# Output weights loaded in 4 KB rows, four matrix rows to a partition, with selection matmuls ahead of the output product

## The chip, the cores and the metric

The kernel runs on one core of a Trainium2 chip. The metric is the device time of one execution in microseconds (us). Before the change it is 1385.94 us, the median of three runs (1384.96 to 1386.25).

## The reference, cut to what matters

Two attention operators for one new token, batch 4, head size 128, outputs side by side:

```python
# A: 32 query heads on 8 key/value heads, the last W = 2048 of 8192 keys of the cache
q = x @ wq                      # 4 x 512 by 512 x 4096
p = softmax(q . k / sqrt(128))  # per batch and head
o = p @ v
out_A = o.reshape(4, 4096) @ wo # wo: 4096 x 512, bf16
# B: the same with 32 query heads on 32 key/value heads and 8192 keys
out = concatenate([out_A, out_B], axis=-1)   # 4 x 1 x 1024
```

Nearly all of the bytes are the caches of B: 2 x 4 x 32 x 8192 x 128 elements of 2 bytes, 537 MB of the 588 MB that the kernel reads. The two `wo` matrices, which the change is about, are 4.2 MB each.

## The kernel before

The work is cut into 72 chunks: 8 of A (one for each key/value head; K and V 2 MB each) and 64 of B (two heads of one batch; K and V 4 MB each). For each chunk TensorE transposes K in groups of eight tiles, multiplies them with q, and later multiplies the probabilities with V. One queue issues all loads in a fixed order: K of the next chunk, V of this one, and a `wo` piece of four heads (512 KB) where one is due. A load is issued when its place in memory is free. A `wo` piece goes into one of three slots:

```python
def dma_wo(i):
    ab, wg = (0, i) if i < Hkv else (1, i - Hkv)
    slot = i % NWO                                   # NWO = 3
    src = WO[ab][wg * 4 * P:(wg + 1) * 4 * P, :].rearrange("(hl d) n -> d hl n", d=P)
    dst = wor[:, slot, :].rearrange("p (hl n) -> p hl n", hl=4)
    waits = [("wos" if i - NWO >= Hkv else "fin", wo_last[i - NWO])] if i >= NWO else []
    sch.add_dma("sp", lambda e: e.dma_start(dst, src), "d_wo%d" % slot, waits=waits, key=("wo", i))
```

In this form partition d gets row d of each of the four heads, in four rows of 1 KB. The output product can then use a head's output as it lies:

```python
def emit_fin(c):
    ...
    if ab == 1:
        ov = oz[:, :].rearrange("p (b u) -> p b u", u=2)
        ops = [(ov[:, :, u], wos[:, u, :]) for u in range(2)]
    else:
        ...
        ops = [(ov[:, :, cc], w[:, cc, :]) for cc in range(REP)]   # REP = 4
    ...                                      # one 512-column matmul for each of ops, into fin
```

Where the product stands among the groups of the next chunks:

```python
def keys_part(c):
    ...
    for g in range(ch["NG"]):                # 8 groups in A, 16 in B
        emit_T(ch["s"] + g)                  # eight transposes; VectorE or ScalarE copies them out
        if g >= SLAG:
            emit_S(ch["s"] + g - SLAG)       # eight score matmuls
        if 1 <= c <= NCA and g == 2:
            stats_gmax(c - 1)
        if 1 <= c <= NCA and g == 3:
            stats_exp(c - 1)                 # VectorE, then ScalarE: exponentials
        if 1 <= c <= NCA and g == 6:
            norm_sum(c - 1)
        if 2 <= c <= NCA + 1 and g == 4:
            emit_fin(c - 2)                  # A: four matmuls
        ...
        if c > NCA + 2 and (c - NCA) % 2 == 1 and g == 4:
            emit_fin(c - 2)                  # B: two matmuls
```

Of the kernel before, what the change touches and what calls it, by code (L numbers as in the profile page):

```python
# [9 lines left out]
BF16 = mybir.dt.bfloat16  # L10
# [12 lines left out]
LASTV = (64, 32, 16, 16)  # L23

TRM0, BC0, L0, Q0, XT0 = 0, 256, 288, 320, 448


class _Sched:
# [88 lines left out]
def bass_concat_heads__sliding_block_cached__mha_block_cached__decode_kernel(  # L117
# [53 lines left out]
    with ExitStack() as es:  # L171
# [7 lines left out]

        kv = sb("kv", [P, NH, 8192], BF16)  # L180
        kt = sb("kt", [P, NKT, TG * P], BF16)
        wos = sb("wos", [P, 2, DO], BF16)
        qb = sb("qb", [P, 2, NW], BF16)
        wor = sb("wor", [P, NWO, 4 * DO], BF16)
        xs = sb("xs", [NB, 2, D], BF16)
# [27 lines left out]

        semnames = ["eng_pe", "eng_dve", "eng_act", "eng_pool", "d_x0", "d_x1", "d_o0", "d_o1"]
        semnames += ["d_h%d" % i for i in range(NH)] + ["d_vl%d" % i for i in range(len(LASTV))]
        semnames += ["d_wo%d" % i for i in range(NWO)]
        sems = {n: es.enter_context(nc.semaphore(n)) for n in semnames}


# [40 lines left out]
        def dma_wo(i):  # L260
            ab, wg = (0, i) if i < Hkv else (1, i - Hkv)
            slot = i % NWO
            src = WO[ab][wg * 4 * P:(wg + 1) * 4 * P, :].rearrange("(hl d) n -> d hl n", d=P)
            dst = wor[:, slot, :].rearrange("p (hl n) -> p hl n", hl=4)
            waits = [("wos" if i - NWO >= Hkv else "fin", wo_last[i - NWO])] if i >= NWO else []
            sch.add_dma("sp", lambda e: e.dma_start(dst, src), "d_wo%d" % slot, waits=waits, key=("wo", i))

# [34 lines left out]
        wo_next = 0  # L302
        for kind, c in loads:
            dma_kv(kind, c)
            if kind == "v":
                while wo_next < NWOL and wo_first[wo_next] <= c:
                    dma_wo(wo_next)
                    wo_next += 1
# [47 lines left out]

        idv = identf[:, :].rearrange("p (x b) -> p b x", b=NB)
        sch.add("dve", lambda e: e.tensor_reduce(out=mk[:, :], in_=idv, axis=AX.X, op=ALU.add), waits=["c_identf"], key="mk")


        def tile_of(kind, c, j):
# [183 lines left out]

        def emit_wos(c):

            h = 2 * chunks[c]["hp"] % 4
            w = wor[:, chunks[c]["wo"] % NWO, :].rearrange("p (hl n) -> p hl n", hl=4)
            sch.add("dve", lambda e: e.tensor_copy(wos[:, :, :], w[:, h:h + 2, :]),  # L550
                    waits=[("wo", chunks[c]["wo"])] + ([("fin", c - 2)] if c - 2 >= NCA else []), key=("wos", c))

        def emit_fin(c):
            ch = chunks[c]
            ab = ch["ab"]
            p0 = 0 if ab == 1 else 32
            if ab == 1:
                ov = oz[:, :].rearrange("p (b u) -> p b u", u=2)
                ops = [(ov[:, :, u], wos[:, u, :]) for u in range(2)]
                waits = [("oT", c), ("wos", c)]  # L560
            else:
                w = wor[:, ch["wo"] % NWO, :].rearrange("p (hl n) -> p hl n", hl=4)
                ov = oT[:, c % NSM, :].rearrange("p (u c) -> p u c", c=REP)
                ops = [(ov[:, :, cc], w[:, cc, :]) for cc in range(REP)]
                waits = [("oT", c), ("wo", ch["wo"])]
            lastc = NC - 1 if ab == 1 else NCA - 1
            for i, (l, r) in enumerate(ops):
                pe_mm(fin[p0:p0 + NB, :], l, r, start=i == 0 and c == 0, stop=i == len(ops) - 1 and c == lastc,
                      waits=waits if i == 0 else [], key=("fin", c) if i == len(ops) - 1 else None)
            if c == lastc:  # L570
                sch.add("dve", lambda e: e.tensor_copy(outsb[p0:p0 + NB, :], fin[p0:p0 + NB, :]), waits=[("fin", c)], key=("osb", ab))
                sch.add_dma("sp" if ab == 1 else "act",
                            lambda e: e.dma_start(out[:, 0, ab * DO:(ab + 1) * DO], outsb[p0:p0 + NB, :]),
                            "d_o%d" % ab, waits=[("osb", ab)], key=("out", ab))
# [6 lines left out]
        def keys_part(c):  # L581
            ch = chunks[c]
            if c >= NCA and (c - NCA) % 2 == 0:
                sch.mark()
            for g in range(ch["NG"]):
                emit_T(ch["s"] + g)
                if g >= SLAG:
                    emit_S(ch["s"] + g - SLAG)
# [4 lines that stand above are left out]
                    stats_exp(c - 1)  # L593
                if 1 <= c <= NCA and g == 6:
                    norm_sum(c - 1)
                if 2 <= c <= NCA + 1 and g == 4:
                    emit_fin(c - 2)
                if c > NCA + 1 and (c - NCA) % 2 == 0 and g == 4:
                    emit_wos(c - 1)
                if c > NCA + 1 and (c - NCA) % 2 == 0 and g == 6:  # L600
                    norm_sum(c - 1)
                if c > NCA + 2 and (c - NCA) % 2 == 1 and g == 4:
                    emit_fin(c - 2)

        def values_part(c, nxt):
# [31 lines left out]
                pe_mm(fin[0:NB, :], qb[:, 0, 0:NB], pbt[0][:, 1, 0:DO], stop=False, waits=["c_qb", ("c_pb", 0)])  # L637
            values_part(c - 1 if c else None, c)
        sch.mark()
        emit_wos(NC - 1)  # L640
        norm_sum(NC - 1)
        for g in range(chunks[NC - 1]["NG"]):
            emit_pv(NC - 1, g)
# [58 lines left out]
```

## Time and profile before

| | before |
|---|---|
| time, median of 3 | 1385.94 us |
| span of the profiled execution | 1384.5 us |
| bytes, mean rate | 587.80 MB, 425 GB/s |
| last K block lands | 1358.60 us |
| from there to the end | 25.9 us |

The views that bound the kernel stand in the prediction. The page's line of busy times adds how much room the engines have:

```profile
PE 1173.0 (85%) x26769; PEld 1130.0 (82%) x26769; DVE 643.2 (46%) x1326; ACT 436.1 (31%) x649; POOL 4.1 (0%) x14
```

TensorE is at 85%. It is no bound over the whole run.

### The profile page before, as it was taken

How to read it: one execution, taken by the hardware profiler on the slowest of the kernel's cores; microseconds unless marked ns; L12 is line 12 of the kernel's file. 1: busy time of each engine (PE TensorE's matmuls, PEld its weight loads, DVE VectorE, ACT ScalarE, POOL GpSimd, SP SyncE). 2: the span in 40 equal slices, each digit the busy share in tenths (PEclk: the TensorE clock that was granted, in tenths of full speed). 3: DMA queues.
4: the chain of work that ended last, by engine and by line, in shares of the span. 5: the costliest groups of instructions: out<-in, count | busy, mean ns of one | idle time of the engine just before them, and what ended most of it. 6: DMA issues, size and time to landing. Idle time of an engine off the chain costs nothing.

```text
span 1384.5 us, 57099 instructions
## 1 busy us (share of the span) xinstructions
PE 1173.0 (85%) x26769; PEld 1130.0 (82%) x26769; DVE 643.2 (46%) x1326; ACT 436.1 (31%) x649; POOL 4.1 (0%) x14
## 2 busy tenths in 40 slices
PE   4888888898888788988889788888898888888888
PEld 4777878897888788887889788887798888887887
DVE  1566444454444444444444444444454445444443
ACT  1554323333223322332233233332233233322332
POOL 1000000000000000000000000000000000000000
PEclk9899999999999999999999999999999999999998
DMA  9999999999999999999999999999999999999996
GB/s 400 414 417 422 426 428 430 434 425 437 427 436 427 432 430 434 429 425 436 427 436 427 435 427 436 426 428 435 429 434 430 433 427 435 428 429 432 431 434 255
DMA packets 29979, 587.80 MB, mean 425 GB/s; under 512 B 2656, under 2 KB 10864, under 8 KB 11120
## 3 DMA queue, kind: packets, MB, share of 16 engines
q1 hardware_dynamic: 29912, 587.22, 99.2%
q8 instruction: 27, 0.44, 0.1%
q14 instruction: 16, 0.13, 0.0%
q10 hardware_dynamic: 24, 0.01, 0.0%
HBM read 587.21 MB, written 0.01 MB: 424 GB/s over the span
## 4 chain that ended last, share of the span: by engine, by line
DMA 66%; PE 31%; DVE 1%; issue 1%; ACT 0%; SPq 0%; ACTq 0%; DVEq 0%
DMA kv<-in_B_k_cache_dram 64%; PE tr L321 19%; PE sc L323 9%; DMA kv<-in_B_wq_dram 2%; PE fin L323 2%; PE po L323 1%; PE ms L323 1%; DVE sA L430 1%; DVE kt L383 0%; DVE rm L439 0%; DVE sA L428 0%; ACT pba L493 0%; PE ms L321 0%; ACT kt L381 0%; ACT pbb L478 0%
## 5 line engine op out<-in xcount | busy, mean ns | idle before, releaser
L321 PE MATMUL tr<-identb,kv 128*128 128x128 bf16 x8704 | 702.7, 231 | 171.7 <-DMA kv<-in_B_k_cache_dram 169.0
L383 DVE COPY kt<-tr 128x1024 bf16<-128x1024 bf16 x736 | 502.6, 691 | 484.5 <-PE tr L321 480.4
L321 PEld LDWEIGHTS tr<-identb,kv 128*128 128x128 bf16 x8704 | 557.7, 105 | 197.4 <-issue 128.6
L381 ACT ACTIVATE kt<-tr 128x1024 bf16<-128x1024 bf16 x352 | 360.2, 1024 | 638.1 <-PE tr L321 635.0
L323 PE MATMUL sc<-qb,kt 128*128 128x64 bf16 x8192 | 424.6, 197 | 1.7 <-issue 1.5
L323 PEld LDWEIGHTS sc<-qb,kt 128*128 128x128 bf16 x8192 | 350.8, 101 | 3.9 <-issue 1.6
L323 PE MATMUL po<-pbb,kv 128*128 128x64 bf16 (+1 forms) x8192 | 289.9, 192 | 5.5 <-issue 5.5
L323 PEld LDWEIGHTS po<-pbb,kv 128*128 128x128 bf16 x8192 | 263.3, 97 | 7.6 <-issue 5.8
L478 ACT ACTIVATE pbb<-sc,negb 64x128 bf16<-64x128 f32 x128 | 51.2, 400 | 296.8 <-DVE negb L468 296.0
L444 DVE TENSOR_REDUCE rm<-sc 64x1 f32<-64x128 f32 x128 | 37.0, 289 | 94.2 <-PE sc L323 93.3
L456 DVE TENSOR_REDUCE gm<-ms 1x2 f32<-1x128 f32 (+1 forms) x72 | 20.1, 279 | 44.6 <-PE ms L321 44.5
L468 DVE COPY negb<-ms 128x1 f32<-128x1 f32 (+1 forms) x72 | 11.4, 159 | 55.4 <-PE ms L323 55.4
L323 PE MATMUL sc<-qs,kt 128*128 128x64 bf16 (+3 forms) x512 | 26.6, 198 | 10.8 <-DVE kt L383 10.5
L323 PEld LDWEIGHTS sc<-qs,kt 128*128 128x128 bf16 x512 | 21.8, 102 | 13.2 <-DVE kt L383 11.8
L323 PE MATMUL ms<-identf,gx 1*128 1x1 f32 (+1 forms) x144 | 27.8, 260 | 0.6 <-DVE gx L460 0.6
L323 PEld LDWEIGHTS ms<-identf,gx 1*128 1x128 f32 (+1 forms) x144 | 21.7, 188 | 4.9 <-DVE gx L460 0.8
L478 ACT ACTIVATION_READ_ACCUMULATOR pbb<-sc,negb 64x1 f32 x128 | 23.7, 185 | 0.0
L321 PE MATMUL ms<-identf,rm 128*1 128x128 f32 (+1 forms) x72 | 19.8, 275 | 0.2 <-DVE rm L444 0.2
L323 PE MATMUL fin<-wos,oz 128*4 128x512 bf16 x64 | 19.5, 386 | 0.3 <-DVE oz L542 0.3
L323 PE MATMUL po<-pba,kv 128*128 128x64 bf16 x512 | 18.9, 193 | 0.0
L460 DVE TENSOR_SCALAR gx<-gm 1x128 f32<-1x128 f32 (+1 forms) x72 | 15.9, 221 | 2.5
L323 PEld LDWEIGHTS po<-pba,kv 128*128 128x128 bf16 x512 | 16.6, 98 | 0.0
(47 smaller groups left out, 155.5 us busy)
## 6 DMA issues: line engine op xcount, KB each, us to landing
kv<-in_B_k_cache_dram SPq DMA_DIRECT2D x64, 4096.0 KB, 27.7
kv<-in_B_v_cache_dram SPq DMA_DIRECT2D x63, 4096.0 KB, 32.5
kv<-in_A_k_cache_dram SPq DMA_DIRECT2D x8, 2048.0 KB, 27.4
kv<-in_A_v_cache_dram SPq DMA_DIRECT2D x8, 2048.0 KB, 26.6
kv<-in_A_wq_dram SPq DMA_DIRECT2D x1, 4096.0 KB, 12.3
kv<-in_B_wq_dram SPq DMA_DIRECT2D x1, 4096.0 KB, 27.3
wor<-in_A_wo_dram SPq DMA_DIRECT2D x8, 512.0 KB, 23.6
wor<-in_B_wo_dram SPq DMA_DIRECT2D x8, 512.0 KB, 33.6
```

The lines of the kernel that those rows point to most:

```text
L321: emit = lambda e: e.transpose(o, l, r)
L323: emit = lambda e: e.matmul(o, l, r, start=start, stop=stop)
L381: sch.add("act", lambda e: e.activation(dst, src, ACTF.Copy), waits=waits, key=("ev", s))
L383: sch.add("dve", lambda e: e.tensor_copy(dst, src), waits=waits, key=("ev", s))
L430: emit = lambda e, src=src, b=b: e.scalar_tensor_tensor(out=t, in0=src, scalar=mk[:, b:b + 1], in1=t, op0=ALU.mult, op1=ALU.add)
L444: sch.add("dve", lambda e, src=src, pp=pp: e.tensor_reduce(out=rm[pp, m, 0:1], in_=src, axis=AX.X, op=ALU.max), waits=[("S", ch["s_last"]) ...
L456: sch.add("dve", lambda e: e.tensor_reduce(out=gm[0:C, m, 0:U], in_=src, axis=AX.X, op=ALU.max), waits=[("trm", c)], key=("gmax", c))
L460: sch.add("dve", lambda e: e.tensor_scalar(out=dst, in0=gv, scalar1=-scale, scalar2=None, op0=ALU.mult), waits=[("gmax", c)], key=("gx", c))
L468: sch.add("dve", lambda e: e.tensor_copy(negb[:, m, 0:C], ms[:, col:col + C]), waits=[("bc", c)], key=("negb", c))
L478: sch.add("act", lambda e, src=src, pp=pp, n=n, u=u: e.activation(pbv[pp, :, u], src, ACTF.Exp, bias=negb[pp, m, 0:1], scale=scale, accum_ ...
```

## The change

The intent: `wo` in rows of 4 KB instead of 1 KB, so that the same bytes cost fewer packets. Partition p then holds rows 4p to 4p+3 of a piece of four heads, so a partition no longer belongs to one position within a head. The head outputs are put in that order by four selection matmuls (0/1 matrices built from the identity) and small VectorE copies. The diff, cut to its core:

```diff
+        wos = sb("wos", [P, 4, DO], BF16)        # was [P, 2, DO]
+        wol = sb("wol", [P, 2, DO], BF16)
+        selm = sb("selm", [P, 4, P], BF16)
+        zs = sb("zs", [P, 3, 16], BF16)
 ...
-            src = WO[ab][wg * 4 * P:(wg + 1) * 4 * P, :].rearrange("(hl d) n -> d hl n", d=P)
-            dst = wor[:, slot, :].rearrange("p (hl n) -> p hl n", hl=4)
+            src = WO[ab][wg * 4 * P:(wg + 1) * 4 * P, :].rearrange("(p r) n -> p (r n)", r=4)
+            dst = wor[:, slot, :]
 ...
+            if (kind, c) == ("k", NC - 4):       # the last two heads once more, in the old form
+                sch.add_dma("sp", lambda e: e.dma_start(wol[:, :, :], ...), "d_wl", key="wol")
 ...
+        def emit_sel(c):
+            ...
+            for r in range(4):
+                pe_mm(ms[:, Z0 + r * n:Z0 + (r + 1) * n], selm[:, r, :], src, ...)
+            ...                                  # B: a memset of the other 64 partitions of zs
+            for k, (h, x) in enumerate(heads):   # A: four copies of 32 partitions, B: two
+                ...
+                sch.add("dve", lambda e, src=src, dst=dst: e.tensor_copy(dst, src), ...)
 ...                                              # emit_fin: four matmuls from zs in A and in B,
 ...                                              # the last chunk as before, from wol
-                if 2 <= c <= NCA + 1 and g == 4:
+                if 2 <= c <= NCA + 1 and g == 5:
+                    emit_sel(c - 2)
+                if 2 <= c <= NCA + 1 and g == 7:
                     emit_fin(c - 2)
 ...
-                if c > NCA + 2 and (c - NCA) % 2 == 1 and g == 4:
+                if c > NCA + 2 and (c - NCA) % 2 == 1 and g == 2:
+                    emit_sel(c - 2)
+                if c > NCA + 2 and (c - NCA) % 2 == 1 and g == 5:
                     emit_fin(c - 2)
```

In A the product moves from group 4 to group 7, the last of a chunk's eight groups, and in B from group 4 to group 5.

More of the change, by code (lines that the diff above doesn't have):

```diff
@@ L25 @@
 TRM0, BC0, L0, Q0, XT0 = 0, 256, 288, 320, 448
+Z0 = Q0
 class _Sched:
@@ L181, in bass_concat_heads__sliding_block_cached__mha_block_cached__decode_kernel @@
         kt = sb("kt", [P, NKT, TG * P], BF16)
-        wos = sb("wos", [P, 2, DO], BF16)
+        wos = sb("wos", [P, 4, DO], BF16)
+        wol = sb("wol", [P, 2, DO], BF16)
+        selm = sb("selm", [P, 4, P], BF16)
+        zs = sb("zs", [P, 3, 16], BF16)
         qb = sb("qb", [P, 2, NW], BF16)
@@ L215, in bass_concat_heads__sliding_block_cached__mha_block_cached__decode_kernel @@
         semnames += ["d_h%d" % i for i in range(NH)] + ["d_vl%d" % i for i in range(len(LASTV))]
-        semnames += ["d_wo%d" % i for i in range(NWO)]
+        semnames += ["d_wo%d" % i for i in range(NWO)] + ["d_wl"]
         sems = {n: es.enter_context(nc.semaphore(n)) for n in semnames}
@@ L304, in bass_concat_heads__sliding_block_cached__mha_block_cached__decode_kernel @@
             dma_kv(kind, c)
+            if (kind, c) == ("k", NC - 4):
+                sch.add_dma("sp", lambda e: e.dma_start(wol[:, :, :], WO[1][(HB - 2) * P:, :].rearrange("(hl d) n -> d hl n", d=P)),
+                            "d_wl", key="wol")
             if kind == "v":
@@ L358, in bass_concat_heads__sliding_block_cached__mha_block_cached__decode_kernel @@
         sch.add("dve", lambda e: e.tensor_reduce(out=mk[:, :], in_=idv, axis=AX.X, op=ALU.add), waits=["c_identf"], key="mk")
+        for r in range(4):
+            i_ = bass.AP(identb[:, :].tensor, identb[:, r:r + 1].offset, [identb[:, :].ap[0], [0, 4], [4, 32]])
+            sch.add("dve", lambda e, r=r, i_=i_: e.tensor_copy(selm[:, r, :].rearrange("p (x y) -> p x y", x=4), i_),
+                    waits=["c_identb"], key="selm" if r == 3 else None)
         def tile_of(kind, c, j):
@@ L546, in emit_wos @@
         def emit_wos(c):
-            h = 2 * chunks[c]["hp"] % 4
             w = wor[:, chunks[c]["wo"] % NWO, :].rearrange("p (hl n) -> p hl n", hl=4)
-            sch.add("dve", lambda e: e.tensor_copy(wos[:, :, :], w[:, h:h + 2, :]),
+            sch.add("dve", lambda e: e.tensor_copy(wos[:, :, :], w),
                     waits=[("wo", chunks[c]["wo"])] + ([("fin", c - 2)] if c - 2 >= NCA else []), key=("wos", c))
+        def emit_sel(c):
+            ab, hp = chunks[c]["ab"], chunks[c].get("hp", 0)
+            src, n = (oT[:, c % NSM, :], 16) if ab == 0 else (oz[:, :], 8)
+            for r in range(4):
+                pe_mm(ms[:, Z0 + r * n:Z0 + (r + 1) * n], selm[:, r, :], src,
+                      waits=[("oT", c), "selm"] + ms_read if r == 0 else [], key=("sm", c) if r == 3 else None)
+            t = c % 2 if ab == 0 else 2
+            waits = [("sm", c)] + ([("fin", c - 2)] if c - 2 >= (0 if ab == 0 else NCA) else [])
+            if ab == 1:
+                h0 = 2 * (hp % 2)
+                q = slice(64 - 32 * h0, 128 - 32 * h0)
+                sch.add("dve", lambda e: e.memset(zs[q, t, :], 0.0), waits=waits)
+            heads = [(h, h) for h in range(4)] if ab == 0 else [(h0 + u, u) for u in range(2)]
+            for k, (h, x) in enumerate(heads):
+                pp = slice(32 * h, 32 * h + 32)
+                src = ms[pp, Z0:Z0 + 4 * n].rearrange("p (r b x) -> p r b x", r=4, b=NB)[:, :, :, x]
+                dst = zs[pp, t, :].rearrange("p (r b) -> p r b", r=4)
+                sch.add("dve", lambda e, src=src, dst=dst: e.tensor_copy(dst, src), waits=waits,
+                        key=("zs", c) if k == len(heads) - 1 else None)
+            ms_read[:] = [("zs", c)]
         def emit_fin(c):
@@ L556, in emit_fin @@
             p0 = 0 if ab == 1 else 32
-            if ab == 1:
+            if c == NC - 1:
                 ov = oz[:, :].rearrange("p (b u) -> p b u", u=2)
-                ops = [(ov[:, :, u], wos[:, u, :]) for u in range(2)]
-                waits = [("oT", c), ("wos", c)]
-            else:
-                w = wor[:, ch["wo"] % NWO, :].rearrange("p (hl n) -> p hl n", hl=4)
-                ov = oT[:, c % NSM, :].rearrange("p (u c) -> p u c", c=REP)
-                ops = [(ov[:, :, cc], w[:, cc, :]) for cc in range(REP)]
-                waits = [("oT", c), ("wo", ch["wo"])]
+                ops = [(ov[:, :, u], wol[:, u, :]) for u in range(2)]
+                waits = [("oT", c), "wol"]
+            elif ab == 1:
+                ops = [(zs[:, 2, 4 * r:4 * r + 4], wos[:, r, :]) for r in range(4)]
+                waits = [("zs", c), ("wos", c)]
+            else:
+                w = wor[:, ch["wo"] % NWO, :].rearrange("p (r n) -> p r n", r=4)
+                ops = [(zs[:, c % 2, 4 * r:4 * r + 4], w[:, r, :]) for r in range(4)]
+                waits = [("zs", c), ("wo", ch["wo"])]
             lastc = NC - 1 if ab == 1 else NCA - 1
@@ L639, in bass_concat_heads__sliding_block_cached__mha_block_cached__decode_kernel @@
         sch.mark()
-        emit_wos(NC - 1)
         norm_sum(NC - 1)
```

## The prediction

> **What bounds the kernel now.** I read the page's slices first, then its DMA part, then the waits of the load queue, then the chain of waits at the end of the run.
>
> ```profile
> PE   4888888898888788988889788888898888888888
> DVE  1566444454444444444444444444454445444443
> DMA  9999999999999999999999999999999999999996
> GB/s 400 414 417 422 426 428 430 434 425 437 427 436 427 432 430 434 429 425 436 427 436 427 435 427 436 426 428 435 429 434 430 433 427 435 428 429 432 431 434 255
> DMA packets 29979, 587.80 MB, mean 425 GB/s; under 512 B 2656, under 2 KB 10864, under 8 KB 11120
> q1 hardware_dynamic: 29912, 587.22, 99.2%
> ```
>
> The DMA row is full in every slice but the last, and the load queue's packets alone fill 99.2% of the 16 engines' span. The kernel streams 588 MB and is bound by that stream. The GB/s row adds a detail: slices 2 to 4, in which eight of the sixteen output-weight (wo) loads fall, move 400 to 422 GB/s, and later slices about 432. Of the packets, 10864 - 2656 = 8208 lie between 512 B and 2 KB; the trace's list of packets gives them all 1024 B, and 8192 = 16 loads x 512 are the wo rows.
>
> Next: does the stream wait for the program anywhere? In turn: waits of the load queue (us in total, times, longest), the only one of TensorE (PE) from 200 to 1370 us, and two rows of the DMA issues (the last column is the median time from issue to landing).
>
> ```profile
> SPq L291 <- PE sc L323: 901.7, 62, 21.8
> ...
> SPq L266 <- PE fin L323: 32.3, 6, 6.0
> ```
>
> ```profile
> PE tr L321 <- DMA kv<-in_B_k_cache_dram: 163.1, 59, 6.0
> ```
>
> ```profile
> kv<-in_B_k_cache_dram SPq DMA_DIRECT2D x64, 4096.0 KB, 27.7
> ...
> wor<-in_A_wo_dram SPq DMA_DIRECT2D x8, 512.0 KB, 23.6
> ```
>
> The queue's 901.7 us of waiting look bad and are harmless. A K load of 4.19 MB needs 9.7 us at 432 GB/s but lands 27.7 us after its issue, so about 18 us of older loads lie ahead of it whenever it is issued. TensorE, for its part, waits 163.1/59 = 2.8 us at each K landing: it has slack in the second operator's 64 chunks, and the DMA has none.
>
> Last, the end of the chain, in order of time (start, us, what):
>
> ```profile
> 1330.88 27.72 DMA kv<-in_B_k_cache_dram
> 1358.60 0.05 issue
> 1358.65 2.10 PE tr L321 x24
> ...
> 1363.36 0.52 PE fin L323 x2
> ...
> 1377.46 3.27 PE po L323 x128
> ...
> 1381.04 1.03 PE fin L323 x2
> 1382.07 0.02 issue
> 1382.09 0.68 DVE outsb L571
> ```
>
> The run ends a fixed stretch of compute after the last K block lands: 1384.5 - 1358.6 = 25.9 us, TensorE busy for 22.2 of them. So time = landing of the last K (pure DMA) + this tail (compute), and the change touches both.
>
> **What the Trainium skill says.** "DMA: Bandwidth & Descriptors", section "Why small descriptors are slow (HBM only)", gives a fixed cost per packet of about 3 cycles on top of one cycle per 32 B: 35 against 32 for 1 KB, 131 against 128 for 4 KB, so four 1 KB packets cost 140/131 = 7% more than one of 4 KB. The trace agrees in kind and shows about twice the size (16%, next part). "Perfetto Trace Analysis", section "DMA Optimizations", names transfers under 2 KB as those with significant overhead; the 400 GB/s slices agree. "VectorE: DVE Perf Modes", section "The perf-mode tier table", gives 693 ns for an SBUF copy of 2048 bf16 elements per partition; this trace has only 1024 elements, 418 ns.
>
> **The change, part by part.**
>
> 1. *1 KB rows become 4 KB rows (removes).* Median packet durations in the trace, by size: 1024 B 46 ns, 4096 B 159 ns (the last V pieces), 16384 B 613 ns, 32768 B 1216 ns. They lie on one line: (1216 - 159)/28672 = 0.0369 ns per byte plus 8 ns per packet. Four 1 KB packets take 184 ns, one of 4 KB 159: 25 ns saved, 2048 times, over 16 engines = 3.2 us. With the means (48.9 and 160.3 ns) it would be 4.5 us. As a check without durations: counting packets in 40 us stretches, a stretch with one wo load moves 0.12 MB (0.27 us) less than one without; the same load at 4 KB should still lose (159.5 x 128 - 16 x 1216)/16 = 0.06 us, so 0.21 us x 16 = 3.4 us. I take **-3.4 us**.
> 2. *A second copy of the last two heads' rows (adds).* The new tile wol is loaded early, 256 KB in the old form: 256 packets x 46 to 49 ns / 16 = **+0.8 us** on the DMA. It is issued ahead of the last K block, so it counts in full.
> 3. *Selection matmuls and copies (adds).* Eight chunks of the first operator and 31 of the second get 4 small matmuls each: 156. The 31 also use four instead of two 512-column matmuls: +62. At the chain's step of 0.52/2 = 0.26 us for a 512-column one, and about 0.06 us for a small one (8 sc steps take 0.43 us just after a DMA wait), a second-operator pair of chunks gains 4 x 0.06 + 2 x 0.26 = 0.8 us of TensorE against 2 x 2.8 = 5.6 us of waiting. Hidden. VectorE (DVE) gains a 64-partition memset, two 32-partition copies (about 0.16 us each, as the 158 ns negb copies) and 693 - 418 = 0.28 us on the wos copy: about 0.75 us in a pair of 39 us, with VectorE under half busy. Hidden.
> 4. *The last chunk is the exception*, since its key part lies in the tail: the selection and the four-row product of the pair before are issued there: 4 x 0.06 + 2 x 0.26 = **+0.75 us**. The wos copy that goes from the end (0.42 us, beside the exponentials) was not on the chain: 0.
> 5. *Later release in the first operator (moves).* The product moves from group 4 to group 7 of a chunk, some 2.5 us later, and the next wo load and the K behind it wait for it (the 32.3 us row). With 18 us or more queued, this starves nothing.
>
> Sum: -3.4 + 0.8 + 0.75 = -1.85 us; 1385.9 - 1.9 = **1384.0 us**.
>
> **The rivals.** (a) *The full small-packet penalty returns.* If the low 400 to 417 GB/s of the first slices were all owed to the wo rows and came back to 430, 138 us x 4% = 5 us would be saved: 1381. Against it: those slices also hold the start-up and 16 KB rows (613 ns, 2% dearer per byte than 32 KB rows), which stay. (b) *TensorE or VectorE takes over in the first operator.* There TensorE waits for almost no DMA (3.3 us at the first K of the second operator), and 8 x (0.25 us of selection + some waiting for the copies) could use that up; releases come later on top. If the DMA ran dry for it, +2 to +5 us: 1387 to 1389. For it: VectorE is at 6 tenths there. Against it: the 23.6 us to landing, so 20 us of delay would be needed, not 3. (c) *The tail grows more than I count*: TensorE's clock dips after each wait (24 transposes take 2.10 us in the last chunk, 1.51 us in the one before), and the selection sits just there. That is worth perhaps 0.5 us. (d) *A large gain* (over 2%, 28 us) is impossible from 1.4% of the bytes, the 8.4 MB of wo.
>
> **Range and chances.** Parts 1, 2 and 4 may be off by about 1 us each; the three runs before spread over 1.3 us. Rivals (a) and (b) widen both sides: 1381.5 to 1386.5. Faster by over 2%: 0.01; within 2%: 0.98; slower: 0.01, for a stall I don't see.
>
> **What would show it.** Packets under 2 KB fall from 10864 to 10864 - 8192 + 256 = 2928 (some more for added semaphore writes), the bytes rise by 0.26 MB, and slices 2 to 4 gain 5 to 10 GB/s. The DMA row stays full. The last K lands 2 to 3 us earlier, near 1356; from there to the end it takes 26.5 us instead of 25.9, with four fin matmuls in the last key part. TensorE's wait at each K shrinks from 2.8 to about 2.4 us. A DMA row with a gap near 90 to 135 us would prove rival (b); a last K no earlier than before would mean that the packets' fixed cost was hidden already; 4 KB packets well above 160 ns would undo part 1.

## More of the kernel before

TensorE's program is straight-line code for A and the first two chunks of B. From chunk 10 on, it is a loop over pairs of chunks:

```python
def loop(first, end):
    return nc.Fori(first, end, 1, engines=type(mybir.ALL_ENGINES)([pe]), head_slot={pe: 0})
sch.emit_looped("pe", e, sems, loop)
```

## The result, and the profile after

| | before | after |
|---|---|---|
| median of 6 runs, same rounds | 1385.49 us (1384.87 to 1386.31) | 1387.01 us (1385.12 to 1389.36) |
| ratio after/before | | 1.0011, 95% interval 0.9998 to 1.0024 |
| span of the profiled execution | 1384.5 us | 1384.2 us |
| last K block lands | 1358.60 us | 1357.95 us |
| from there to the end | 25.9 us | 26.3 us |

A ratio is the mean time of one kernel's fast runs over that of the other's of the same rounds, so it is not quite the ratio of the medians. The predicted gain of 1.9 us is not there, and the median lies above the range. The page after:

```profile
PE 1187.7 (86%) x26987; PEld 1137.2 (82%) x26987; DVE 670.0 (48%) x1454; ACT 435.4 (31%) x649; POOL 4.1 (0%) x14
DMA  9999999999999999999999999999999999999995
GB/s 401 424 422 432 423 415 426 437 425 436 428 435 429 433 430 433 431 430 432 432 432 432 431 430 434 430 431 432 432 431 432 432 431 431 433 430 433 432 426 247
DMA packets 24109, 588.09 MB, mean 425 GB/s; under 512 B 2672, under 2 KB 2944, under 8 KB 5248
q1 hardware_dynamic: 24040, 587.48, 99.0%
```

The packets fell as planned (2944 under 2 KB). Slices 2 to 4 rose from 414, 417 and 422 GB/s to 424, 422 and 432. But slice 6, which is 173 to 208 us, fell from 428 to 415 GB/s. That is the first sign: one slice has 3% less, and a slice is 34.6 us, so about 1 us is missing there. The DMA row still shows a 9 for it, because 9 stands for anything from 90% up.

The waits of the load queue (us in total, times, longest), with lines that answer to those of before:

```profile
SPq L296 <- PE sc L331: 898.0, 62, 18.8
...
SPq L271 <- PE fin L331: 73.0, 6, 19.8
```

The wait of a `wo` load for its slot, which the prediction called the 32.3 us row, is now 73.0 us, the longest 19.8 instead of 6.0. TensorE's wait for K from 200 to 1370 us, and two rows of the DMA issues:

```profile
PE tr L329 <- DMA kv<-in_B_k_cache_dram: 142.3, 56, 4.7
```

```profile
kv<-in_B_k_cache_dram SPq DMA_DIRECT2D x64, 4096.0 KB, 26.7
...
wor<-in_A_wo_dram SPq DMA_DIRECT2D x8, 512.0 KB, 18.7
```

142.3/56 is 2.5 us a wait, where 2.4 were predicted. The `wo` loads of A land 18.7 us after their issue instead of 23.6: less was queued ahead of them, so the queue is shorter. The end of the chain (start, us, what):

```profile
1332.24 25.70 DMA kv<-in_B_k_cache_dram
...
1357.99 2.74 PE tr L329 x24
1360.73 0.30 PE sc L331 x8
1361.03 0.08 PE ms L331 x4
...
1363.17 0.95 PE fin L331 x4
...
1380.71 1.03 PE fin L331 x2
```

**Where the time went.** I summed the trace's list of packets into bytes delivered up to each moment and compared the two kernels, in us at 431 GB/s. After leads before by 2.0 us at 160 us and by 1.96 us at 195 us. At 205 us the lead is 0.50 us and at 240 us 0.48 us. So the change gains about 2 us in the first operator and loses 1.5 us of it within 10 us. The stretch from 197 to 203 us in both kernels (window, length, busy time of PE, PEld, DVE, ACT, POOL, then granted TensorE clock, DMA share, GB/s):

```profile
197.00:203.00 6.00, 4.15 (x58) 4.04 (x58) 1.17 (x4) 0.91 (x4) 0.00 (x0) 0.72 1.02 437
```

```profile
197.00:203.00 6.00, 4.96 (x143) 4.86 (x141) 2.32 (x4) 1.76 (x2) 0.00 (x0) 1.00 0.85 336
```

The first is before, the second after: the DMA is full in one and at 0.85 with 336 GB/s in the other. In steps of 1 us from 198 us on, 16.0, 12.0, 9.0, 10.5 and again 16.0 of the 16 DMA engines are busy after the change. The load queue ran dry. This is the prediction's rival (b), at 200 us instead of 90 to 135 us. The experiments ask why.

### The profile page after: what moved, and what is told of

It reads as the page before. It is cut to its first block, busy times and chain, and to the rows that moved or that the text cites. A ratio compares the mean times of both kernels' runs of the same rounds, so it can differ in the third digit from the quotient of the medians.

```text
span 1384.2 us, 57666 instructions
## 1 busy us (share of the span) xinstructions
PE 1187.7 (86%) x26987; PEld 1137.2 (82%) x26987; DVE 670.0 (48%) x1454; ACT 435.4 (31%) x649; POOL 4.1 (0%) x14
## 2 busy tenths in 40 slices
DMA packets 24109, 588.09 MB, mean 425 GB/s; under 512 B 2672, under 2 KB 2944, under 8 KB 5248
## 4 chain that ended last, share of the span: by engine, by line
DMA 56%; PE 38%; DVE 3%; issue 1%; ACT 1%; SPq 0%; ACTq 0%; DVEq 0%
DMA kv<-in_B_k_cache_dram 54%; PE tr L329 22%; PE sc L331 10%; PE po L331 3%; PE fin L331 3%; DMA kv<-in_B_wq_dram 2%; PE ms L331 1%; DVE sA L444 1%; DVE kt L397 1%; DVE rm L453 0%; DVE sA L442 0%; DVE zs L584 0%; DVE sA L500 0%; ACT eA L504 0%; DVE rs L511 0%
## 5 line engine op out<-in xcount | busy, mean ns | idle before, releaser
L329 PE MATMUL tr<-identb,kv 128*128 128x128 bf16 x8704 | 702.5, 232 | 150.8 <-DMA kv<-in_B_k_cache_dram 142.3
L331 PE MATMUL sc<-qs,kt 128*128 128x64 bf16 (+3 forms) x512 | 26.4, 197 | 13.6 <-DVE kt L397 13.3
L331 PE MATMUL fin<-wos,zs 128*4 128x512 bf16 x124 | 31.8, 378 | 0.0
L563 DVE COPY wos<-wor 128x2048 bf16<-128x2048 bf16 x31 | 21.2, 684 | 0.0
## 6 DMA issues: line engine op xcount, KB each, us to landing
wor<-in_A_wo_dram SPq DMA_DIRECT2D x8, 512.0 KB, 18.7
```

The lines of the kernel that those rows point to most:

```text
L329: emit = lambda e: e.transpose(o, l, r)
L331: emit = lambda e: e.matmul(o, l, r, start=start, stop=stop)
L563: sch.add("dve", lambda e: e.tensor_copy(wos[:, :, :], w), waits=[("wo", chunks[c]["wo"])] + ([("fin", c - 2)] if c - 2 >= NCA else []), k ...
```

## The experiments

Thirteen kernels ran, in four rounds. The texts name theories by letters; here is what each stands for.

- **A, instruction supply.** The extra matmuls shift the place of TensorE's code, and TensorE stalls for instructions at the entry of its loop.
- **B, late release.** The selection and the later product in the first operator release the `wo` slots late, and the load queue with them.
- **C, VectorE.** The small copies of the selection make each chunk of the first operator longer.
- **D, clock in the tail.** What decides the last us is whether TensorE runs the tail at half clock, after the wait for the last K.
- **E, the product's place.** Moving the product from group 4 to group 7 lengthens a chunk of the first operator by itself.

What pointed to A is TensorE's timeline at the loop's entry. Each line has start, length and what ran; in brackets the idle time just ahead of it and what ended it. Before, then after:

```profile
158.57 2.74 PE L321 MATMUL tr<-identb,kv 128*128 128x128 bf16 x24 [2.62 <-DMA kv<-in_B_k_cache_dram]
```

```profile
164.78 2.52 PE L329 MATMUL tr<-identb,kv 128*128 128x128 bf16 x22 [6.15 <-issue]
```

Before, TensorE waits for a K block. After, it waits 6.15 us for nothing that the profile shows. The trace also has packets of 16 KB of instructions (I take them for TensorE's), one about every 7.4 us up to some 200 us. One more follows near 240 us and one in the tail; apart from those two the repeating loop fetches none.

### Round 1: e1 to e4

**e1_head64** moves the loop's first instruction by 64 places within its block of instructions.

```diff
-  return nc.Fori(first, end, 1, ..., head_slot={pe: 0})      # after
+  return nc.Fori(first, end, 1, ..., head_slot={pe: 64})
```

> The changed kernel with the TensorE loop's first instruction placed at slot 64[...] instead of slot 0; nothing else. Theory A (the added selection matmuls push the code ahead of the loop past a block boundary, the loop head moves one block on, and entering the loop waits about 6 us for an instruction fetch that queues behind the loads): the 6.15 us stall near 158 us falls under 1.5 us, the DMA row has no gap near 200 us, the time is about 1383.5 us, ratio to before 0.9985. Theory B (the first operator is simply slower with its selections, copies and later releases): no effect, 1386 to 1387 us, ratio 1.0005 to 1.001.

Measured: 1385.03 us (1383.93 to 1386.67), before 1386.26 on the same chip, ratio 0.9993 [0.9979, 1.0007]. The stall at the entry is gone; the longest stall left around it is 2.92 us. The lead falls from 2.03 to 1.09 us by 240 us, a loss of 0.9 instead of 1.5. So A seems to have a part in it, not the whole: this is one trace, and two traces of the changed kernel itself lose 1.5 and 2.0 us (e11, below).

**e2_pad** puts five matmuls without use into each chunk of the first operator of the kernel before, so that the code is longer but the product stays where it was.

```diff
+  if 2 <= c <= NCA + 1 and g == 5:                            # before
+      for r in range(5):
+          pe_mm(ms[:, Q0 + 16 * r:Q0 + 16 * r + 16], identb[:, :], identb[:, 0:16], ...)
```

> The kernel before plus five small matmuls in each of the first operator's eight later chunks, whose result nobody reads: 80 more TensorE instructions ahead of the loop, no copies, no other loads, no later release. Theory A: the loop head moves one fetch block on, a stall of about 6 us at the loop's entry (2.6 us of idle before), the loads behind it late by 4 to 6 us, time 1385.5 to 1386.5 us, ratio 1.000 to 1.001, with a small gap of the DMA near 200 us. Theory B: no stall beyond the wait for the K block, ratio 1.000.

Measured: 1386.16 us (1385.19 to 1386.41), ratio 1.0000 [0.9986, 1.0014]. The stall appears, made from nothing but the code's length:

```profile
164.44 2.74 PE L321 MATMUL tr<-identb,kv 128*128 128x128 bf16 x24 [3.92 <-issue]
```

The fourth K issue of the second operator past 130 us comes at 197.64 us instead of 192.72. Yet the DMA stays full: the bytes delivered differ from before by less than 0.1 us all the way to 240 us. The small gap that was expected there did not come: stalls of this size alone do not make the queue run dry.

The lateness is not all idle time. TensorE from 130 to 200 us, in before, e2 and after (columns as in the stretch from 197 to 203 us above):

```profile
130.00:200.00 70.00, 57.97 (x1328) 55.23 (x1324) 31.84 (x64) 20.13 (x29) 0.00 (x0) 0.94 1.01 429
```

```profile
130.00:200.00 70.00, 56.98 (x1278) 54.20 (x1274) 30.99 (x62) 20.12 (x29) 0.00 (x0) 0.90 1.01 429
```

```profile
130.00:200.00 70.00, 55.94 (x1195) 53.22 (x1193) 31.81 (x67) 20.18 (x30) 0.00 (x0) 0.88 1.00 424
```

TensorE is idle for 12.0, 13.0 and 14.1 us, so e2 idles only 1.0 us more than before. But the granted clock fell from 0.94 to 0.90 and 0.88, which over 70 us is the work of 2.8 and 4.2 us at full clock. The trace's list of granted clocks shows where: half clock from 157.3 us on for 10.24 us in e2 and from 159.3 us on for 10.24 us in after, against 3.41 us in before. The seven traces with a stall of 3.9 us or more at the loop's entry (after, e2, e4, e5, e6, e11, e13) all have a half-clock stretch of 10.24 us there, the eight others none longer than 6.83 us. So below, "instruction stalls" means the stalls and the half clock around them; no run separates the two.

**e3_rows_only** takes only the 4 KB rows. Its output is wrong, which doesn't matter for the time. (The product pairs wrong rows.)

```diff
-  src = WO[ab][...].rearrange("(hl d) n -> d hl n", d=P)      # before
-  dst = wor[:, slot, :].rearrange("p (hl n) -> p hl n", hl=4)
+  src = WO[ab][...].rearrange("(p r) n -> p (r n)", r=4)
+  dst = wor[:, slot, :]
```

> The kernel before with the wo loads alone changed to 4 KB rows, the compute left as it is (so the result is wrong on purpose). It measures the DMA part by itself. Prediction's part 1: 3.4 us saved, 1382.1 us, ratio 0.9975. If the fixed cost per packet were hidden behind other queues: ratio 1.000.

Measured: 1381.50 us (1381.38 to 1382.77), ratio 0.9971 [0.9958, 0.9985]. The lead grows to 1.98 us at 180 us, stays there, and is 3.57 us at 1355 us; the last K lands at 1355.12 us, 3.5 us earlier. The DMA part of the prediction (-3.4 us) is right. The rest of the 5 us is the tail: 24.4 us instead of 25.9 (theory D, below).

**e4_early_release** moves the selection to group 2 and the product back to group 4, so that the slots come free as early as before the change.

```diff
-  if 2 <= c <= NCA + 1 and g == 5: emit_sel(c - 2)            # after
-  if 2 <= c <= NCA + 1 and g == 7: emit_fin(c - 2)
+  if 2 <= c <= NCA + 1 and g == 2: emit_sel(c - 2)
+  if 2 <= c <= NCA + 1 and g == 4: emit_fin(c - 2)
```

> The changed kernel with the first operator's selection at group 2 and its product at group 4 again (instead of 5 and 7), so that wo slots and the K loads behind them are released some 2.5 us earlier; the number of instructions is the same. Theory B: the DMA gap near 200 us shrinks or goes, about 1384.5 us, ratio 0.9993. Theory A: the stall of about 6 us at the loop's entry stays, and so does the gap, 1386 to 1387 us, ratio 1.0005 to 1.001.

Measured: 1390.79 us (1388.41 to 1393.20), ratio 1.0034 [1.0020, 1.0047]: worse than either kernel, a miss. Chunks of the first operator now take 12.7 to 13.0 us. By the program's order the copies of the selection now stand ahead of the exponentials' part of the statistics on VectorE; that this is the reason was not tested by itself. The fourth K issue comes at 205.39 us, and the DMA runs dry twice. The first time, from 180 us on:

```profile
180.00:190.00 10.00, 7.76 (x220) 7.51 (x216) 3.90 (x9) 2.05 (x2) 0.00 (x0) 1.00 0.74 288
```

It loses 5.3 us by 240 us. So lateness of the K issues costs time, but "earlier in the group order" is not "earlier in time".

### Round 2: e5 to e8

**e5_one_copy** replaces the four 32-partition copies of the selection in the first operator by one of 128 partitions. It takes one head's columns for all four, which is wrong on purpose (the difference still passed the comparison).

```diff
-  heads = [(h, h) for h in range(4)] if ab == 0 else ...      # after
-  pp = slice(32 * h, 32 * h + 32)
+  heads = [(0, 0)] if ab == 0 else ...
+  pp = slice(32 * h, 32 * h + 32) if ab == 1 else slice(0, P)
```

> The changed kernel with one 128-partition copy in place of four 32-partition copies after each selection of the first operator (it takes head 0 for all, so the result is wrong on purpose); instruction counts of TensorE unchanged. Theory C (the first operator's chunks now last 12.14 us, longer than their loads of about 11 us, because VectorE's four copies lie in the loop of TensorE and VectorE; the load queue then runs dry near 200 us): three copies of 0.17 us less give chunks of about 11.6 us, the gap of 1.5 us near 200 us goes, time 1383 to 1384.5 us, ratio 0.998 to 0.999. If only the instruction fetch counts: chunks may shorten, but gap and time stay, ratio 1.001.

Measured: 1385.72 us (1385.01 to 1390.04), ratio 1.0008 [0.9994, 1.0022]. The chunk still takes 12.14 us, as in the changed kernel, against 11.08 us for a chunk of before that has no half clock in it. C falls as the cause of the longer chunk: with the copies gone, the chain of waits runs over ScalarE's work for the probabilities (1.70 us) and its eviction (0.92 us) instead.

**e6_act_first** moves the first of a chunk's eight K evictions in the first operator from VectorE to ScalarE and the second one the other way; **e7_act_first_head64** has that and the loop's place of e1; **e8_before_act_first** is the kernel before with that eviction order, as a control.

```diff
-  if (g % 3 == 2) if c >= NCA else (g % 2 == 1):              # e6, e7: after; e8: before
+  if (g % 3 == 2) if c >= NCA else g in (0, 3, 5, 7):
```

> The changed kernel, with the first eviction of each first-operator chunk moved from VectorE (busy with the score selection then) to ScalarE and the second one to VectorE. Theory C: the chunk falls from 12.14 to about 11 us, at or under its load time, TensorE waits for a K block again at the first K of the second operator, no DMA gap, time 1383 us, ratio 0.9975 to 0.9985. If only the instruction fetch counts: ratio 1.0005 to 1.001.

> The run before this one and the loop head at slot 64 together. Theory C: nothing left to gain from the loop head once the queue no longer runs dry, so the same as e6_act_first within 0.5 us. If the fetch at the loop's entry still costs: 1 us less than e6_act_first.

> The kernel before with the same move of the first eviction to ScalarE. Its queue never runs dry, so both theories expect no change: 1385.5 to 1386.3 us, ratio 1.000, though its first-operator chunks may get shorter and TensorE may wait longer for K blocks.

Measured, beside before at 1386.19 us: e6 1385.48 us (1383.61 to 1387.08), ratio 1.0002; e7 1386.08 us (1384.94 to 1386.23), ratio 1.0000; e8 1385.09 us (1384.52 to 1386.51), ratio 1.0000. The intervals are about 0.0014 to either side, so the times tell nothing. The traces do. The chunk shrank only to 12.03 us in e6 and e7 (10.98 in e8). But the fourth K issue came at 197.19 us in e6 and at 192.27 us in e7, and the loss fell to 0.65 us in e6 and to nothing in e7:

```profile
197.00:203.00 6.00, 5.30 (x92) 5.15 (x92) 1.45 (x6) 0.91 (x4) 0.00 (x0) 0.72 1.01 434
...
1358.00:1366.00 8.00, 8.00 (x119) 7.25 (x117) 4.05 (x9) 2.05 (x2) 0.00 (x0) 0.71 0.91 381
```

e6 and e7 differ in the place of the loop's code alone, which makes them the cleanest pair for theory A: with it the stall at the loop's entry is 5.66 us and 0.65 us are lost, without it nothing is. It is one trace each.

The first of these e7 lines shows a full DMA where after had 0.85. The second shows why the time of e7's profiled execution (1386.13 us) is no better: in the tail the granted clock averages 0.71 over 8 us. The tail took 27.6 us.

### Round 3: e9 to e11

**e9_warm_after** is e7 with 18 matmuls without use ahead of each wait for K in the second operator. **e10_warm_before** is the kernel before with the same 18. **e11_after_again** is the changed kernel, unaltered, for a second trace.

```diff
+  if c >= NCA + 2:                                            # e9: e7; e10: before
+      for r in range(18):
+          pe_mm(ms[:, Q0:Q0 + 192], identb[:, :], qs[:, 0:192], waits=ms_read if r == 0 else [])
```

> The changed kernel with the first eviction on ScalarE, the loop head at slot 64 (as e7_act_first_head64, which delivered its loads 2.7 us ahead of the kernel before and yet ended only 0.3 us earlier, with a tail of 27.6 us from the last K block at half clock for 6.8 us of it), and 18 matmuls whose result nobody reads ahead of each K wait of the loop, about 1.5 us of TensorE. Theory D (the tail after the last K block is run at half clock for 3.4 or 6.8 us whenever TensorE waited about 3.7 us just before it; that eats the gain): the last chunk starts at full clock, the tail is about 25 us, time 1383.3 us, ratio 0.998. If the tail's length has another cause: 1385.5 to 1386 us, ratio 1.000.

> The kernel before with the same 18 matmuls ahead of each K wait of the loop. Its times fall in two groups 1.4 us apart, near 1384.9 and 1386.3. Theory D: the upper group goes, all runs near 1384.8 us, tail 24.3 us instead of 25.9. If the groups have another cause: both stay, 1386 us.

> The changed kernel as it is, once more, for a second trace. Its six runs spread over 4.2 us, the ones before over 1.4. The first trace lost 1.55 us of deliveries near 200 us and 1.4 us in the tail at half clock. If both vary from run to run (how long the queue is dry, how many 3.4 us slots at half clock fall in the tail), this trace shows other sizes of the two and the time follows from them: 1385 to 1389.5 us, median 1386.5 to 1387.5.

Measured, beside before at 1386.17 us (1384.65 to 1388.00): e9 1383.74 us (1383.74, 1383.67, 1385.15, 1383.64, 1385.08), ratio 0.9988 [0.9974, 1.0001]; e10 1386.26 us (1386.11 to 1386.52), ratio 1.0002 [0.9988, 1.0015]; e11 1386.70 us (1385.18 to 1387.56), ratio 1.0002 [0.9988, 1.0015]. e11 repeats the dry stretch: its lead falls from 1.93 us at 180 us to nothing at 240 us. e9 gives the right result and has the lowest median of all correct kernels, though its interval still touches 1.

The last wait of TensorE for K, and what followed it, in e9 and then in e10:

```profile
1356.85 1.51 PE L329 MATMUL tr<-identb,kv 128*128 128x128 bf16 x24 [2.21 <-DMA kv<-in_B_k_cache_dram]
```

```profile
1358.49 1.63 PE L321 MATMUL tr<-identb,kv 128*128 128x128 bf16 x24 [2.24 <-DMA kv<-in_B_k_cache_dram]
```

The wait was shortened in both, to 2.2 us. e9 then had no half clock until 1376.3 us, 5.4 us before its end (tail 25.0 us). e10 had half clock from 1359.7 to 1363.2 us, a tail of 25.8 us, and none of the faster runs that were expected. So the length of that wait does not decide it, and that part of D falls. What stands is that such slots of 3.4 us exist and what each costs. All kernels run their last 3.5 to 6.4 us at half clock, where little is left to compute, so I count only the slots that start in the part before 1366 us. Sorted by that number, the traces give:

| half-clock slots in the tail | kernels of before's type: tail | kernels of after's type: tail |
|---|---|---|
| none | e3 24.4, e8 24.3, e12 24.4 us | e6 25.0, e9 25.0 us |
| one | before 25.9, e2 25.9, e10 25.8 us | after 26.3, e11 26.4, e5 26.5, e13 26.3, e4 26.5 us |
| two | | e1 27.5, e7 27.6 us |

A slot goes with 1.2 to 1.5 us more, and the changed tail itself costs 0.6 us more than the old one. The granted clock (the column before the last two) over the same 8 us of before, after and e3:

```profile
1358.00:1366.00 8.00, 7.35 (x117) 6.87 (x118) 3.54 (x6) 2.05 (x2) 0.00 (x0) 0.79 0.95 404
```

```profile
1358.00:1366.00 8.00, 8.00 (x133) 7.25 (x134) 4.42 (x9) 2.05 (x2) 0.00 (x0) 0.83 0.98 415
```

```profile
1358.00:1366.00 8.00, 8.00 (x180) 7.51 (x178) 4.95 (x8) 3.50 (x4) 0.00 (x0) 1.00 0.86 359
```

e3 issued 180 matmuls where before issued 117. This also fits the two groups of times that the kernel before shows, near 1384.9 and near 1386.3 us; its own lower group was not traced. Of its relatives with a full DMA, the two that were traced without a slot ran in 1385.09 and 1384.71 us (e8, e12), the two with one slot in 1386.28 and 1386.23 us (e2, e10).

### Round 4: e12 and e13

**e12_before_fin_late** moves only the product of the kernel before, from group 4 to group 7. **e13_sel3_fin5** is the changed kernel with selection and product at groups 3 and 5.

```diff
-  if 2 <= c <= NCA + 1 and g == 4: emit_fin(c - 2)            # e12: before
+  if 2 <= c <= NCA + 1 and g == 7: emit_fin(c - 2)

-  ... g == 5: emit_sel(c - 2)    ... g == 7: emit_fin(c - 2)  # e13: after
+  ... g == 3: emit_sel(c - 2)    ... g == 5: emit_fin(c - 2)
```

> The kernel before with the first operator's product moved from group 4 to group 7 of a chunk, and nothing else: old loads, no selection, no copies, the same number of instructions. Theory E: its chunks grow from 11.08 us (at full clock) to about 12 us, the load queue waits for wo slots 70 us instead of 32; with 64 instructions fewer ahead of the loop than the changed kernel the queue just holds or loses up to 1 us, ratio 1.000 to 1.001. If the selections and copies make the chunk long: 11.1 us, waits as before, ratio 1.000.

> The changed kernel with the first operator's selection at group 3 and its product at group 5 (5 and 7 as changed, 2 and 4 in e4_early_release, which was worse). Theory E: chunks of about 11.5 us, the loss of deliveries near 200 us falls from 1.6 us to under 0.5 us, time 1385 us, ratio 0.999. If the place of the product does not matter: 12.1 us or more, and 1386.5 us.

Measured, beside before at 1385.06 us (1384.70 to 1387.47): e12 1384.73 us (1384.56 to 1386.37), ratio 0.9996 [0.9982, 1.0009]; e13 1385.96 us (1385.15 to 1386.57), ratio 1.0002 [0.9988, 1.0015]. e13 is a miss: its chunks take 12.03 us where 11.5 were expected, and it loses 1.35 us by 240 us. e12 settles the chunk's length. The products in the chain of waits, for e3 (the product where it was), e12 and after:

```profile
62.16 0.96 PE fin L323 x4
73.23 0.96 PE fin L323 x4
```

```profile
66.77 0.96 PE fin L323 x4
78.91 0.96 PE fin L323 x4
```

```profile
66.71 0.96 PE fin L331 x4
78.85 0.96 PE fin L331 x4
```

The distance is 11.07 us in e3, and 12.14 us in e12 and in after. The step of 1.07 us is about the product's own 0.96 us. At group 4 the product filled a time in which TensorE had to wait for the softmax statistics on VectorE and ScalarE. At group 7 it stands among work that follows without a wait, so it adds its full length to each chunk. The selection matmuls are not needed for it. (Where the product stood among the groups between was not mapped: at group 5, in e13, the chunk takes 12.03 us.) In before itself the five distances from 52 to 110 us go from 11.08 to 12.14 us, 11.65 on average, since half-clock slots fall into them; e12's average there is 12.22 us. A chunk of the first operator brings 4.72 MB, 11.15 us at 423 GB/s: at 11.07 us TensorE just keeps up with the DMA, at 12.14 us it does not. TensorE's waits from 30 to 135 us, before and in e12 (us in total, times, longest), show that its slack there is gone:

```profile
PE tr L321 <- DMA kv<-in_B_k_cache_dram: 3.3, 1, 3.3
```

```profile
PE sc L323 <- DVE kt L383: 15.5, 15, 1.6
...
PE tr L321 <- DMA kv<-in_B_k_cache_dram: 0.5, 1, 0.5
```

And yet e12 does not run dry: its lead stays within 0.1 us of zero.

### The runs together: how deep the queue was

The last view puts all traces side by side. At an issue of K, the bytes of all earlier loads less the bytes already delivered on the load queue are what is still queued. I divided by 431 GB/s. "Late" is the issue time of the fourth K past 130 us, against 192.72 us before. "Lost" is the fall of the lead from its value at 180 to 195 us to that at 240 us.

| kernel | 4th K issued | late | queued then | queued at the next K | lost |
|---|---|---|---|---|---|
| before | 192.72 | 0 | 10.9 us | 11.0 us | - |
| e3 | 191.85 | -0.9 | 9.8 | 11.3 | 0 |
| e8 | 193.88 | +1.2 | 9.8 | 8.7 | 0 |
| e10 | 194.54 | +1.8 | 9.1 | 7.6 | 0 |
| e7 | 192.27 | -0.5 | 9.4 | 9.0 | 0 |
| e12 | 195.14 | +2.4 | 8.5 | 9.7 | 0 |
| e9 | 195.02 | +2.3 | 6.6 | 5.2 | 0 |
| e2 | 197.64 | +4.9 | 6.1 | 6.0 | 0 |
| e6 | 197.19 | +4.5 | 4.6 | 4.0 | 0.65 us |
| e5 | 198.67 | +6.0 | 3.2 | 5.0 | 0.7 |
| e1 | 199.50 | +6.8 | 2.3 | 5.2 | 0.9 |
| e13 | 199.14 | +6.4 | 2.6 | 3.3 | 1.35 |
| after | 200.63 | +7.9 | 1.7 | 3.2 | 1.5 |
| e11 | 199.45 | +6.7 | 2.6 | 2.6 | 2.0 |
| e4 | 205.39 | +12.7 | 0.3 | 5.9 | 5.3 |

This is the finding. While more than about 5 us are queued nothing is lost; below that the loss grows. The late product alone goes with 2.4 us of lateness (e12), the instruction stalls alone with 4.9 us (e2). Neither alone takes the queue below 5 us; the changed kernel, which has both, goes far below. That 2.4 and 4.9 make 7.3 of after's 7.9 us is not shown to be more than a coincidence: these are single traces, two traces of one kernel (after, e11) differ by 1.2 us, and e8 and e10, which have neither, are 1.2 and 1.8 us late.

The lateness does not build up chunk by chunk in the first operator. There the K issues of after, between 55 and 105 us, are 2.0 to 3.1 us later than before and no more; the first K past 130 us is late by 0.4 us, the next three by 2.6, 7.1 and 7.9 us. What the longer chunks use up is slack: before, TensorE still waits 3.3 us for the first K of the second operator, in e12 0.5 us, in after not at all. The 7 us come at the loop's entry, with the stalls and the half clock. The gain takes its part too: the DMA runs 2 us ahead of before, the loads are issued at TensorE's pace, so the queue is those 2 us shorter. 10.9 - 7.9 - 1.7 (the lead at 200 us) makes 1.3 us; the count gives 1.7.

Why 5 us and not zero: in the dry stretch 9 to 12 of 16 engines are busy, so the engines were not equally far, and the first run out while the mean still has work. The trace supports this: it lists sixteen completion updates for every load. For the fourth K of before they spread over 6.9 us, from 2.5 us ahead of the moment at which the byte count has the block delivered to 4.4 us after it. For the third K of after, issued at 177.6 us, the first update is 2.1 us ahead. If each update is one engine's (the trace does not name the engine), that is some 2 of the 5 us. Another 1.1 us pass between an issue and its first packet, as the first load of before shows (0.81 to 1.86 us). The rest is not explained.

## Why the prediction was wrong, point by point

- **Part 1, -3.4 us: right.** e3 has 3.57 us more delivered at 1355 us, and its last K lands 3.5 us earlier. The 4 KB packets take 161 ns.
- **Part 2, +0.8 us: right by the byte count.** e7 and e9, which do not run dry, lead by 3.31 us, of which 0.61 us are the extra 0.26 MB themselves. Against e3's 3.57 us that is 0.9 us. Their last K lands 1.4 to 1.7 us after e3's, though; the other 0.6 to 0.8 us stay open. A K block has landed when the slowest engine is done, which a byte count does not see.
- **Part 3, hidden: right** for the loop. TensorE's waits for K shrank from 2.8 to 2.5 us, and the wos copy takes 684 ns, where the prediction took 693.
- **Part 4, +0.75 us: right**, 0.6 us between tails without a half-clock slot.
- **Part 5 is the step that failed**: "With 18 us or more queued, this starves nothing", and with it rival (b)'s "20 us of delay would be needed, not 3". For the stretch that it had in view it was right: between 53 and 105 us 16.8 to 20.2 us were queued before the change (by the count of bytes), the K issues came 2.0 to 3.1 us later, and nothing starved. But it took the 18 us for the depth "whenever it is issued". They were the median time from issue to landing less the block's own transfer. The count gives a median of 12.7 us from 200 us on, and only 10.8 to 14.7 us at the four K issues from 133 to 193 us. The landing is later than the count, because it takes the last of the sixteen updates. And the prediction had no term for the loop's entry: with TensorE's slack gone and its code longer, a stall of 6.15 us and 10.24 us of half clock made the fourth K 7.9 us late. That left 1.7 us queued, and 1.5 us were lost.
- **The tail's clock** (rival c) was put at "perhaps 0.5 us". A slot of half clock goes with 1.2 to 1.5 us, and there are none, one or two. The clock does not dip "after each wait": in before, 35 half-clock stretches begin between 200 and 1370 us, where TensorE waits 59 times for K. As the profiled executions of before and after have one each, it does not explain their difference. It does limit what medians can tell at this size.
- **Readings that do not hold**, none of which moves the sum: the 400 GB/s is slice 1, in which no `wo` piece lands and which stays at 401 after the change; slices 2 to 4 had 414 to 422. The 24 transposes of the chunk before the last took 2.74 us, not 1.51 (that was the chunk before it). 16 KB rows at 613 ns are 0.8% dearer per byte than 32 KB rows at 1216 ns, not 2%.

The sum for the two profiled executions: rows -3.5, second copy +0.9, dry stretch +1.5, and 0.4 us not attributed make the last K 0.65 us earlier (1358.60 to 1357.95). The tail is 0.3 us longer. Together -0.3 us, as in the spans (1384.5 to 1384.2).

What stays open: how the 7.9 us divide between lost slack, stalls and half clock (e12 takes the slack alone and e2 brings the stalls, but no run separates the stalls from the half clock), and the changed kernel's other runs. Its eleven runs, in two rounds, go from 1385.12 to 1389.36 us. Two traces lose 1.5 and 2.0 us, so the size of the dry stretch varies, and e4 shows that it can be 5 us. But no run above 1387 us was traced, so I can't say that the slow ones are long dry stretches. The split between them and half-clock slots is not shown.

## What to carry to other kernels

Before you call a delay harmless because "the queue is deep", count the bytes issued and not yet delivered at that very moment; the time from issue to landing is longer than that. Follow the lateness from load to load until the steady state begins (here 0.4 us at 134 us and 7.9 us at 201 us), and ask of each group of instructions that moves whether it stood in a wait (where it was free) or on the path (where it costs its whole length). The change may still be had: e9, which keeps the 4 KB rows, with another eviction order, another place of the loop's code and 18 extra matmuls ahead of each K, ran in 1383.74 us beside 1386.17 us, with an interval that just touches 1. What the 18 matmuls have to do with it is not shown, as e10 has them too and kept its half-clock slot. At differences of 0.1%, look at the clock of the tail before you believe a median.

## What the Trainium skill lacked or had wrong

- "DMA: Bandwidth & Descriptors", section "Why small descriptors are slow (HBM only)", leads to 7% for four 1 KB packets against one of 4 KB. That is the prediction's estimate from the 3 cycles alone; with the 32 B of descriptor metadata that the section adds for each operation it would be 9%. The trace of after has 46 ns for 1 KB and 161 ns for 4 KB: 184 against 161, 14%. e3's 3.5 us bear the larger figure out: 23 ns for each of the 2048 rows, over 16 engines, are 2.9 us, where 7% would be 1.4 us.
- "Runtime: NRT & Kernel Launch", section "Instruction fetch mechanics", says that instructions are fetched in blocks of 16 KiB (the trace agrees: packets of 16384 B, about one every 7.4 us) and that the cost of crossing a block is "mostly hidden", and it names unrolled code as the way to avoid stalls. Here the stalls lie in and at the end of straight-line code beside a full DMA: up to 6.15 us in after, 3.92 us in e2.
- "TensorE: Matmul & The Clock Gate", section "What's actually happening", gives a window of about 3.4 us at the end of which the clock is halved or restored. The trace agrees with the slot's length (3.41 us, or two to four of them). It says half rate comes after at least one idle window; here slots came after waits of 2.24 us (e10) and 2.39 us (before) and stayed away after 2.21 us (e9). The periods of full clock between slots are whole multiples of that window too: 17.1 or 34.1 us in the second half of before and after, up to 116.05 us in e10.
- I found no page that says how to read the depth of a load queue. Before the change, a K block lands 27.7 us after its issue (median), with its own 9.7 us of transfer and 12.7 us of older bytes ahead of it (median from 200 us on), and engines run dry from about 5 us of queued bytes down.
